# A fused attention and two-layer MLP kernel: another opening, another engine for one copy, and eight weight chunks prepared during attention

## Chip, cores and metric

The kernel runs on one core of one Trainium2 chip. The metric is the device time of one execution in microseconds; the median of three runs of the kernel before is 671.48 us (669.37 to 672.0).

## What is computed

The reference, cut to what matters (B = 2, H = 8, S = 768, D = 64, six hash bits):

```python
q_bits = (einsum('bhsd,dk->bhsk', q, proj) > 0)          # the same for k
mask = q_bucket[:, :, :, None] == k_bucket[:, :, None, :]
scores = where(mask, scale * q @ k.T, -1e9)
attn = softmax(scores); x = (attn @ v), heads side by side # 1536 x 512
h = x @ w_in;  y = (h * tanh(softplus(h))) @ w_out         # 512 -> 2048 -> 512
h = y @ w2_in; s = h * softmax(h)
out = layer_norm(s) * g_ln @ w2_out                        # 512 -> 1024 -> 512
```

The four weight matrices arrive as 64-bit floats. Every product is made of parts (a high part and a rest), so that the result has the precision of 32-bit floats.

## The kernel before

**Stages.** Sixteen heads are handled in eight pairs; each head has six tiles of 128 queries by 768 keys, 96 tiles in all. For a pair, `load_qk` reads q and k, `qk_split` and `qk_rest` (GpSimd) cut them into two parts, `qk_turn` (line 1114, TensorE) transposes them, and `qk_evac` (line 1130) copies them from PSUM into the operand A with ScalarE. q is needed a second time, as the first 64 rows of the operand B: `qk_again` (line 1122) copies the same two PSUM banks again, with ScalarE too, while k's part of B comes by a DMA from A (`qk_copy`). `bits` (TensorE) multiplies A by the projection, whose two parts are the tiles `ph` and `pl`; `signs` (line 1166, VectorE) turns the result into signs, and `bits_in` sends them by DMA into the last 12 rows of B, two DMAs a head. With A and B, `scores` makes four matmuls a tile; then come `row_max`, `row_bias` (VectorE), `exps` (ScalarE), a split and a transposition by DMA or by TensorE, and `weigh`, 18 matmuls with v.

The first pair is special. Its q and k are loaded head by head (`load_first`), and ScalarE (`first_high`) and VectorE (`first_low`) cut them, not GpSimd.

After attention, the first layer runs in 48 units (`up`, 12 matmuls of 512 columns; `mish`, five VectorE operations among others; `down_high` and `down_low`, 12 matmuls). Its tokens come transposed from `turn_x`. Units 0 to 4 use the first ten weight chunks, two a unit. The second layer works on twelve blocks of tokens.

**Weights.** They come in 48 chunks of 512 KB. A chunk is loaded by SP's queue (`w_load`, line 695) into one of two raw buffers, and `w_steps` (line 702) converts it: one ScalarE operation (line 708), four on VectorE (lines 710, 712, 714, 716), then the high part by ScalarE (line 721) and the rest by GpSimd (line 723). The first `nconv=4` chunks have room from the start; the next ones get theirs once the score buffers are given back, that is when attention's scores are made.

**Order.** All five queues have an order fixed at build time. `program_order` lists the operations with what they read and write; each has a cost (`COST`) and a due time (`PHASE`, in tiles); `Order.run` plays a list schedule with them, and the kernel emits the instructions in that order. Each engine then executes its queue strictly in order. Transposed tiles and weight chunks, and the operands A, B, live in rings whose sizes the planner knows: `ns=17` slots of 3 KB a partition for the tiles, `hb=5` operand buffers.

The opening in `program_order`:

```python
for h in range(2):
    for o in range(2):
        dma(("load0", h, o), -200 + h, "load0_", ...)
for i in range(2):
    dma(("const", 1 + i), -200, "const1", (), [("pj", i)])
```

Of the kernel before, what the change touches and what calls it, by code (L numbers as in the profile page):

```python
# [9 lines left out]
F32 = mybir.dt.float32  # L10
# [21 lines left out]
    score=3.35, max=20.58, bias=-41.09, exp=15.90, hi=38.27, lo=17.83, tdma=-17.31, tr0=9.66, thi0=-4.77,  # L32
    tlo0=10.96, tr1=11.10, thi1=34.69, tlo1=-13.57, weigh=18.21, norm0=14.45, norm1=-19.21, norm2=-18.99,
    load=9.76, vload=18.36, split0=-28.52, rest0=7.87, split1=21.38, rest1=13.25, turn=-1.67, evac=-13.71,
    copy=-20.07, bits0=0.84, bits1=5.16, sign=1.45, bdma=18.25, vmax=21.88, vs0=-7.99, vs1=-38.96, vs2=-32.92,
    vs3=2.95, vs4=-18.77, vs5=24.66, vs6=21.48, vs7=18.09, vs8=-29.73, vh=36.55, vl=-0.60, first=-10.47,
    turn_=28.58, evac_=34.57, copy_=-15.70, bits_=16.40, sign_=37.45, bdma_=19.08, vload_=-49.04, vmax_=44.13,
    vs_=-10.86, vh_=21.48, vl_=-28.42, second=83.83, wload=30.72, w0=22.26, w1=-4.27, w2=-0.69, w3=-21.85,
    w4=35.81, w5=1.29, w6=-6.70, wpace=-25.03, wat=161.08, wlate=-523.98, turngap=0.35, x0_=-1.63, x1_=4.53,
    x2_=17.68, load_=-22.95, const0=6.26, begin0=-1.50, vs8_=11.76, outlag=-10.05, up=-22.50, a0=23.29,  # L40
    a1=31.43, a2=29.92, a3=28.02, a4=-26.04, a5=-5.08, a6=25.14, a7=32.44, a8=34.92, a9=-7.34, a10=23.68,
    da=-13.05, db=-11.20, ky0=73.43, ky1=29.52, x0=20.32, x1=-16.34, x2=-11.42, sy0=19.47, sy1=20.33,
    u2=-10.02, n0=23.50, n1=0.20, n2=-4.13, n3=13.94, n4=24.34, n5=19.25, n6=-17.42, n7=-0.19, n8=32.85,
    n9=9.81, n10=14.27, n11=20.09, n12=-5.13, n13=21.63, t2=-30.92, l0=-7.19, l1=7.73, d2=22.76, ot=25.03,
    od=-2.50, wloadL=72.31, w0L=-5.19, w1L=12.35, w2L=42.25, w3L=-36.78, w4L=62.43, w5L=-4.37, w6L=-15.41,
    begin1=-37.18, begin2=-25.15, begin3=-15.47, const1=34.72, const3=-15.20, load0_=6.26,
# [4 lines left out]
    score=0.7, max=0.865, bias=0.14, exp=0.878, hiA=0.733, hiD=0.469, lo=1.596, tr=0.325, thi=0.371, tlo=0.469,  # L51
    weigh=0.533, norm0=0.075, norm1=0.106, norm2=0.469, split=0.915, rest=1.79, turn=0.5,
    evacA=0.691, evacD=0.865, bits=0.69, sign=0.985, vmax=0.87, vs0=0.11, vs1=0.2, vs2=0.11,
    vs=0.07, vs8=0.884, vh=0.733, firstA=0.413, firstD=0.469, w0=0.52, w1=0.602, w2=0.602,
    w3=0.602, w4=0.602, w5=0.52, w6P=1.225, w6D=0.663, x0=0.434, x1=0.478, x2=0.602,
    up=0.68, a0=0.478, a1=0.335, a2=0.602, a3=0.613, a4=0.52, a9=0.52, a10=1.225, da=0.453, db=0.2265,
    sy0=0.52, sy1=0.602, u2=1.36, n0=1.131, n1=1.091, n2=0.069, n3=0.075, n4=1.196, n5=0.069, n6=1.133,
# [13 lines left out]
COLD = 14.0  # L71


class Order:
# [60 lines left out]
    def run(self):  # L135
# [14 lines left out]
        free = dict(BEGIN)  # L150
# [49 lines left out]
        for _ in range(n):  # L200
            best = None
            for e, line in queue.items():
                cand = []
                for r, i in line:
                    r = max(r, free[e])
                    if ops[i][7]:
                        r = ring(i, r)[0]
                        if r is None:
                            continue
                    cand.append((r, due[i], i))  # L210
                if not cand:
                    continue
                first = min(cand)[0]
                pick = min((c for c in cand if c[0] <= first + self.slack), key=lambda c: c[1:])
                if best is None or pick[0] < best[0]:
                    best = (pick[0], e, pick[2])
            at, e, i = best
            o = ops[i]
            queue[e] = [x for x in queue[e] if x[1] != i]
            for tok, name, m, k in ring(i, at)[1]:  # L220
                place[tok] = k
                held[name][k:k + m] = [tok] * m
            for tok in o[7]:
                if tok[0] in taken:
                    taken[tok[0]].append(tok)
            start[i] = at
            if o[8] is not None:
                hw = max(at + 0.05, hw) + o[2]
                begin = max(hw + 0.65, wire)
                wire = done[i] = begin + o[8]  # L230
                if e == "SP":
                    free[e] = begin + 0.85 if o[0][0] == "tdma" else hw
                else:
                    free[e] = at + 0.05
            else:
# [3 lines left out]
                free[e] = done[i] = at + o[2] * (2 if e == "PE" and at < COLD else 1)  # L239
# [28 lines left out]
def program_order(pairs, tiles, routes, evac, chunks, wide, due, rings, stores, slack, queues=(), pooled=0,  # L268
                  gates=(0, 0, 0, 0), early=8, attention_only=False, split="G", again="A"):
# [11 lines left out]
    def start():  # L281
        dma(("const", 0), -200, "const0", (), [("cs",)])
        op(("begin", 0), A, 0.2, -200, "begin0", [("cs",)], [("ident",)])
        for h in range(2):
            for o in range(2):
                dma(("load0", h, o), -200 + h, "load0_", (), [(("r%d", "rr%d")[h] % o, 0)])
        for i in range(2):
            dma(("const", 1 + i), -200, "const1", (), [("pj", i)])
# [12 lines left out]
    def prep(n):  # L301
# [6 lines left out]
        for h in range(2):  # L308
            th = t0 if n else h * due["second"]
            for o in range(2):  # L310
                sp = ("sp%d" % o, n) if n else ("f", o, h)
                if not n:
                    op(("first", 0, h, o), A, COST["firstA"], th, "first", [(("r%d", "rr%d")[h] % o, 0)], [sp])
# [7 lines left out]
                if again and not o:  # L321
                    op(("evac", n, h, 2), A if again == "A" else V, COST["evac" + again], d, "evac" + f, [s],
                       [("B", n, h, 0)])
# [73 lines left out]
    def chunk(i, base, slot, reads):  # L397
# [3 lines left out]
        dma(("wload", i), base, "wload" + q, [("wg", i - 1)] + reads, [wr], 0, (("bdma", 0, (0,), 0, 1),))  # L401
# [171 lines left out]
def lsh_attention_moe_kernel(  # L573
# [15 lines left out]
    nconv=4,  # L589
# [9 lines left out]
    ns=17,  # L599
    early=5,  # L600
    hb=5,
# [8 lines left out]
    again="A",  # L610
# [511 lines left out]
    def qk_again(p, h):  # L1122
        dst = second(p, h, 0)[0:64].rearrange("p (a n) -> p a n", a=2)
        src = two_banks("st", p, h, 0)[0:64, :, 0:NH]
        if again == "A":
# [155 lines left out]

    def const_in(i):
# [23 lines left out]

    nc.gpsimd.memset(ones, 1.0)
# [4 lines left out]
    for w in v_t:  # L1312
        nc.gpsimd.memset(w[:, :, :, 0, D:D + 1], 1.0)
    nc.gpsimd.memset(ph.bitcast(F32), 0.0)
# [7 lines left out]
        bank=(8, dict(s=2, st=2, sb=2, sv=1, t=1, o=1, tx=1, h=1, q=1, wq=1, y0=1, y1=1, y2=1, y3=1, h2=2, t2=2, o2=1)),  # L1322
# [3 lines left out]
                          early, split=split, again=again)  # L1326
    keys = order.run()
    do = dict(
        load=load_qk, load0=load_first, split=qk_split, rest=qk_rest, const=const_in, begin=begin,
# [39 lines left out]
```

## Time and profile before

| what | value |
|---|---|
| median of three runs | 671.48 us |
| the profiled execution's own time | 670.35 us |
| its span, first to last instruction | 668.5 us |
| TensorE busy | 632.3 us (95%) |
| VectorE busy | 540.1 us (81%) |
| ScalarE busy | 445.3 us (67%) |
| GpSimd busy | 338.1 us (51%) |
| mean granted TensorE clock | 0.978 |
| the first score matmul and the last one start at | 18.5 and 222.6 us |

Busy times are of one execution. In the profile PE is TensorE, PEld its weight loads, DVE VectorE, ACT ScalarE, POOL GpSimd and SPq the queue of SyncE, which issues the DMAs. A matmul's recorded length overlaps the next one's, so the distance between the starts of two matmuls is what one takes. A clock of 1.00 is 2.4 GHz and 0.50 is 1.2 GHz.

### The profile page before, as it was taken

Reading aid. Unit: us, or ns where it says so; the run is one execution under the profiler, and the core shown is the slowest. Engines: PE = TensorE matmul, PEld = TensorE weight load, DVE = VectorE, ACT = ScalarE, POOL = GpSimd, SP = SyncE. Lnnn points to the kernel's source line nnn. Section 1 sums busy time; section 2 is a strip of 40 time slices with the busy share of each in tenths; the row PEclk is TensorE's granted clock in tenths of the full one; section 3 lists DMA queues with packets and bytes.
Section 4 is the critical chain, followed back from the end, with each engine's and each line's share of the span. In section 5 each row is a group of like instructions: output and inputs, shape, how many; then the busy total and the mean of one; then the engine's idle time right before and its main releaser. Section 6 shows DMA issues by size and latency. Waiting matters only on the chain.

```text
span 668.5 us, 12185 instructions
## 1 busy us (share of the span) xinstructions
PE 632.3 (95%) x4520; PEld 522.9 (78%) x4520; DVE 540.1 (81%) x1113; ACT 445.3 (67%) x718; POOL 338.1 (51%) x261
## 2 busy tenths in 40 slices
PE   5899899999989988799999999999999999999997
PEld 4788798887978866588777777887778888888886
DVE  3777869788799899999999999999998596545440
ACT  5889989999999856666666666655556265443341
POOL 4678867869568555466666665444566200000000
PEclk9879979999999999989999999999999999999999
DMA  6959869898999943322333221121120000000011
GB/s 173 234 145 178 192 144 181 172 194 163 149 189 190 198 115 122 95 95 73 95 103 95 86 92 60 63 70 56 64 95 1 1 0 18 16 32 17 16 49 48
DMA packets 125148, 68.11 MB, mean 102 GB/s; under 512 B 103584, under 2 KB 118048, under 8 KB 125088
## 3 DMA queue, kind: packets, MB, share of 16 engines
q1 hardware_dynamic: 125088, 67.33, 42.0%
q8 instruction: 35, 0.57, 0.4%
q14 instruction: 25, 0.20, 0.1%
HBM read 34.68 MB, written 3.15 MB: 57 GB/s over the span
## 4 chain that ended last, share of the span: by engine, by line
PE 53%; DVE 19%; ACT 5%; issue 5%; DMA 1%; POOL 1%; ACTq 0%; DVEq 0%; POOLq 0%
PE banks L815 4%; PE banks L817 4%; PE banks L816 4%; PE banks L871 4%; PE banks L872 4%; PE banks L876 4%; PE banks L920 3%; PE banks L924 3%; PE banks L986 3%; PE banks L984 3%; PE banks L921 3%; PE banks L985 3%; DVE mx L1202 3%; PE banks L1195 3%; DVE a L833 2%
## 5 line engine op out<-in xcount | busy, mean ns | idle before, releaser
L1244 POOL TENSOR_TENSOR store<-store 128x768 f16<-128x768 f32 x64 | 104.5, 1651 | 25.5 <-ACT store L1222 23.7
L1202 DVE TENSOR_REDUCE mx<-banks 128x1 f32<-128x768 f32 x96 | 90.5, 950 | 23.8 <-PE banks L1195 22.1
L849 POOL TENSOR_TENSOR n<-c,a 128x512 f32<-128x512 f32 x48 | 62.8, 1308 | 82.7 <-DVE a L845 73.9
L1211 ACT ACTIVATE store<-banks,mx 128x768 f32<-128x768 f32 x96 | 93.7, 995 | 6.4 <-DVE mx L1207 5.0
L815 PE MATMUL banks<-xh,w 128*128 128x512 f32 x192 | 78.7, 410 | 7.0 <-DVE xl L804 4.8
L871 PE MATMUL banks<-gh,w 128*128 128x512 f32 x192 | 76.1, 396 | 4.4 <-ACT gh L854 4.4
L817 PE MATMUL banks<-xh,w 128*128 128x512 f32 x192 | 76.2, 397 | 0.6 <-POOL w L723 0.6
L816 PE MATMUL banks<-xl,w 128*128 128x512 f32 x192 | 76.1, 396 | 0.2 <-DVE xl L804 0.2
L872 PE MATMUL banks<-gh,w 128*128 128x512 f32 x192 | 75.5, 393 | 0.0
L857 POOL TENSOR_TENSOR gl<-n,gh 128x512 fp32r<-128x512 f32 x48 | 62.9, 1309 | 18.9 <-ACT gh L854 18.9
L839 ACT ACTIVATE a<-n,two 128x512 f32<-128x512 f32 x48 | 34.7, 722 | 46.5 <-DVE n L835 46.5
L1262 PE MATMUL banks<-v,store 128*128 128x65 f16 x576 | 61.5, 195 | 3.3 <-DVE store L1239 1.8
L1195 PE MATMUL banks<-A,A 128*128 128x384 f32 x192 | 58.7, 387 | 4.3 <-ACT store L1211 4.1
L723 POOL TENSOR_TENSOR w<-wf,w 128x512 fp32r<-128x512 f32 x40 | 51.7, 1293 | 21.1 <-ACT w L721 20.1
L1264 PE MATMUL banks<-v,store 128*128 128x65 f16 x576 | 61.0, 193 | 0.5 <-DVE store L1239 0.5
L1263 PE MATMUL banks<-v,store 128*128 128x64 f16 x576 | 61.3, 196 | 0.0
L1262 PEld LDWEIGHTS <-store 128*128 128x128 f16 x576 | 53.8, 97 | 6.1 <-issue 4.3
L1263 PEld LDWEIGHTS <-store 128*128 128x128 f16 x576 | 54.1, 98 | 3.0 <-issue 2.6
L1264 PEld LDWEIGHTS <-store 128*128 128x128 f16 x576 | 54.2, 100 | 0.6 <-DVE store L1239 0.6
L876 PE MATMUL banks<-gl,w 128*128 128x512 f32 x192 | 53.7, 391 | 0.0
L1222 ACT ACTIVATE store<-store 128x768 f16<-128x768 f32 x64 | 52.8, 852 | 1.1 <-PE banks L1264 0.9
L815 PEld LDWEIGHTS banks<-xh,w 128*128 128x128 f32 x192 | 36.2, 188 | 21.6 <-DVE a L845 6.7
(123 smaller groups left out, 1715.9 us busy)
## 6 DMA issues: line engine op xcount, KB each, us to landing
wr<-in_moe_w_in_dram SPq DMA_DIRECT2D x24, 512.0 KB
wr<-in_moe_w_out_dram SPq DMA_DIRECT2D x24, 512.0 KB
vr<-in_v_dram SPq DMA_DIRECT2D x8, 384.0 KB
B<-A SPq DMA_DIRECT2D x16, 192.0 KB
out_dram<-ot SPq DMA_DIRECT2D x12, 256.0 KB
q<-in_q_dram SPq DMA_DIRECT2D x7, 384.0 KB
k<-in_k_dram SPq DMA_DIRECT2D x7, 384.0 KB
B<-bits SPq DMA_DIRECT2D x32, 36.0 KB
```

The lines of the kernel that those rows point to most:

```text
L815: nc.tensor.matmul(h, lhsT=wh[:, ks], rhs=xh, start=(kk == 0), stop=False)
L816: nc.tensor.matmul(h, lhsT=wh[:, ks], rhs=xl, start=False, stop=False)
L817: nc.tensor.matmul(h, lhsT=wl[:, ks], rhs=xh, start=False, stop=(kk == KD - 1))
L871: nc.tensor.matmul(y, lhsT=wh[:, os], rhs=g_t[u][0], start=first, stop=False)
L872: nc.tensor.matmul(y, lhsT=wl[:, os], rhs=g_t[u][0], start=False, stop=False)
L876: nc.tensor.matmul(y, lhsT=wh[:, os], rhs=g_t[u][1], start=False, stop=last)
L1202: nc.vector.reduce_max(m[:, 1:2], two_banks("s", t)[:, :, 0:NH], axis=AX.XY, negate=True)
L1211: nc.scalar.activation(kept("e", t).rearrange("p (a n) -> p a n", a=2), two_banks("s", t)[:, :, 0:NH], AF.Exp, bias=m[:, 3:4], scale=m[:, ...
L1244: nc.gpsimd.tensor_tensor(p16[:, 1], kept("e", t), p16[:, 0], op=ALU.subtract)
L1262: nc.tensor.matmul(o, lhsT=pt[:, 0, kc, :], rhs=vh, start=(kc == 0), stop=False)
L1263: nc.tensor.matmul(o[:, 0:D], lhsT=pt[:, 0, kc, :], rhs=vl, start=False, stop=False)
L1264: nc.tensor.matmul(o, lhsT=pt[:, 1, kc, :], rhs=vh, start=False, stop=(kc == NC - 1))
```

## The change

- **Opening.** DMA order: the constants, q and k of head 0, the two copies of the projection, then q and k of head 1. ScalarE may cut head 1's q only after it has begun k's copy of head 0. TensorE first does 20 matmuls of 192 columns on the zeroed tile `ph` (`warm`), for which GpSimd zeroes `ph` first.
- **q's second copy** (`again="VV"`) goes to VectorE for both heads of every pair; in the first pair it is listed behind k's copy.
- **Weights.** `nconv=8`: eight chunks have room from the start. The first four loads (`soon=4`) may be issued behind the loads of pair 1, not only behind the first signs. To make room, `ns` goes from 17 to 15 and `hb` from 5 to 4.
- **Planner.** Nearly all due times are new, some costs are changed by a few per cent, and the time for which the planner counts TensorE as slow goes from 14 to 5 us. So the order of all queues is another one.

```diff
@@ program_order: start, prep, chunk
         for h in range(2):
             for o in range(2):
-                dma(("load0", h, o), -200 + h, "load0_", (), [(("r%d", "rr%d")[h] % o, 0)])
-        for i in range(2):
-            dma(("const", 1 + i), -200, "const1", (), [("pj", i)])
+                dma(("load0", h, o), -200 + h, "load0_", (), [(("r%d", "rr%d")[h] % o, 0)], 0,
+                    [("const", 2)] if h else [])
+            for i in range(0 if h else 2):
+                dma(("const", 1 + i), -200, "const1", (), [("pj", i)], 0, [("load0", 0, 1)])
+        op(("warm",), T, COST["warm"], -200, "warm", [], [("warm", 0)])
...
-                    op(("first", 0, h, o), A, COST["firstA"], th, "first", [(("r%d", "rr%d")[h] % o, 0)], [sp])
+                    op(("first", 0, h, o), A, COST["firstA"], th, "first", [(("r%d", "rr%d")[h] % o, 0)], [sp], 0,
+                       [("evac", 0, 0, 1)] if h else [])
...
-                if again and not o:
-                    op(("evac", n, h, 2), A if again == "A" else V, COST["evac" + again], d, "evac" + f, [s],
+                if again and (o if n == 0 else not o):
+                    g = again[h]
+                    op(("evac", n, h, 2), A if g == "A" else V, COST["evac" + g], d, "evac" + f, [("st", n, h, 0)],
                        [("B", n, h, 0)])
...
-        dma(("wload", i), base, "wload" + q, [("wg", i - 1)] + reads, [wr], 0, (("bdma", 0, (0,), 0, 1),))
+        dma(("wload", i), base, "wload" + q, [("wg", i - 1)] + reads, [wr], 0,
+            (("load", 1, 1) if i < soon else ("bdma", 0, (0,), 0, 1),))
@@ parameters
-    nconv=4,
+    nconv=8,
-    ns=17,
+    ns=15,
-    hb=5,
+    hb=4,
-    again="A",
+    again="VV",
+    soon=4,
@@ new, and the zeroing moved
+    def warm():
+        for _ in range(20):
+            nc.tensor.matmul(bank("warm", 0)[:, 0:192], lhsT=ph[:, 0:128], rhs=ph, start=True, stop=True)
...
+    nc.gpsimd.memset(ph.bitcast(F32), 0.0)
     nc.gpsimd.memset(ones, 1.0)
...
-    nc.gpsimd.memset(ph.bitcast(F32), 0.0)
```

## Rows read from the trace of the kernel before

**Rows 1.** Stages: length, busy of PE, PEld, DVE, ACT, POOL; clock, DMA share, GB/s

```profile
0.00:18.40 18.40, 11.50 (x67) 8.12 (x67) 6.02 (x19) 11.23 (x19) 7.32 (x22) 0.91 0.68 189
18.40:50.00 31.60, 28.68 (x207) 24.41 (x206) 25.60 (x65) 26.21 (x37) 23.85 (x18) 0.84 0.73 181
50.00:100.00 50.00, 46.81 (x554) 41.17 (x551) 37.36 (x105) 45.48 (x63) 39.24 (x27) 0.90 0.87 172
100.00:180.00 80.00, 77.27 (x1033) 68.60 (x1033) 67.20 (x181) 77.34 (x110) 59.01 (x40) 1.00 0.89 175
180.00:222.90 42.90, 39.24 (x581) 35.22 (x579) 41.93 (x108) 42.36 (x63) 30.20 (x19) 1.00 0.97 179
222.90:250.00 27.10, 23.93 (x299) 20.25 (x297) 24.34 (x47) 18.36 (x32) 15.77 (x12) 1.00 0.66 157
250.00:290.00 40.00, 31.89 (x139) 24.06 (x138) 39.39 (x66) 24.83 (x42) 20.80 (x17) 0.96 0.33 105
290.00:410.00 120.00, 119.09 (x507) 93.45 (x505) 117.41 (x192) 76.25 (x130) 78.81 (x62) 1.00 0.29 93
410.00:530.00 120.00, 119.01 (x512) 95.56 (x512) 110.13 (x173) 65.19 (x110) 63.10 (x48) 1.00 0.14 49
```

**Rows 2.** Busy time in two microseconds of the stretch at low clock

```profile
84.00:86.00 2.00, 2.00 (x7) 2.00 (x8) 1.69 (x7) 1.89 (x3) 1.37 (x1) 0.50 1.25 283
```

**Rows 3.** Timeline of the first 19 us (start, length, engine, line, operation)

```profile
2.13 0.43 SPq L1039 DMA_DIRECT2D q<-in_q_dram  x1
...
4.80 1.76 PE L1120 MATMUL banks<-identr,sp 128*128 128x128 f32 x12 [4.80 <-DVE sp L1110]
...
5.67 0.52 ACT L1106 ACTIVATE sp<-q 128x384 fp32r<-128x384 f32 x1 [0.98 <-DMA q<-in_q_dram]
...
8.20 1.49 ACT L1137 ACTIVATE A<-banks 128x768 fp32r<-128x768 f32 x2
...
10.33 0.52 PE L1161 MATMUL banks<-A,ph 128*24 128x384 f32 x1
...
10.65 0.52 PE L1161 MATMUL banks<-A,pl 128*24 128x384 f32 x1
...
11.27 1.06 DVE L1169 TENSOR_SCALAR bits<-banks,cs 24x768 fp32r<-24x768 f32 x1 [1.36 <-PE banks L1161]
...
11.73 0.34 PE L1161 MATMUL banks<-A,ph 128*24 128x384 f32 x1
...
11.91 0.34 PE L1161 MATMUL banks<-A,pl 128*24 128x384 f32 x1
...
12.37 1.70 SPq L1177 DMA_DIRECT2D B<-bits  x2
...
12.96 1.22 PE L1120 MATMUL banks<-identr,sp 128*128 128x128 f32 x12
...
15.67 1.00 PE L1120 MATMUL banks<-identr,sp 128*128 128x128 f32 x6 [1.49 <-POOL sp L1099]
...
18.47 0.97 PE L1195 MATMUL banks<-A,A 128*128 128x384 f32 x2
```

**Rows 4.** Weight loads on SP's queue from 223 to 290 us, first and last

```profile
223.59 0.57 SPq L699 DMA_DIRECT2D wr<-in_moe_w_in_dram  x1
...
284.32 0.34 SPq L699 DMA_DIRECT2D wr<-in_moe_w_out_dram  x1
```

**Rows 5.** Waits between 223 and 292 us (total, times, longest us)

```profile
PE banks L815 <- DVE xl L804: 4.8, 3, 1.8
```

**Rows 6.** Instruction groups: busy us and mean ns behind the bar

```profile
L716 DVE SCALAR_TENSOR_TENSOR wf<-wr,banks 128x512 int32<-128x512 int32 x48 | 32.6, 679 | 0.0
...
L1137 ACT ACTIVATE A<-banks 128x768 fp32r<-128x768 f32 x32 | 25.6, 809 | 8.1 <-PE banks L1120 8.0
...
L1126 ACT ACTIVATE B<-banks 64x768 fp32r<-64x768 f32 x16 | 12.7, 795 | 0.0
...
L1169 DVE TENSOR_SCALAR bits<-banks,cs 48x768 fp32r<-48x768 f32 x7 | 7.4, 1062 | 0.2
```

More of the change, by code (lines that the diff above doesn't have):

```diff
@@ L31 @@
 PHASE = dict(
[L32 to L46, printed above, removed]
+    score=2.89, max=21.69, bias=-20.48, exp=-7.37, hi=37.60, lo=-74.88, tdma=47.79, tr0=9.51, thi0=14.05,
@@ new lines @@
+    tlo0=2.17, tr1=10.84, thi1=28.04, tlo1=16.57, weigh=17.46, norm0=29.45, norm1=6.67, norm2=-77.92,
+    load=19.06, vload=18.96, split0=-188.88, rest0=28.62, split1=-216.02, rest1=37.27, turn=-44.19,
+    evac=-204.06, copy=-27.06, bits0=-103.88, bits1=-136.11, sign=51.37, bdma=40.93, vmax=21.86, vs0=-271.50,
+    vs1=9.08, vs2=-210.73, vs3=-129.45, vs4=-56.64, vs5=-127.12, vs6=-290.81, vs7=144.62, vs8=-328.13,
+    vh=70.16, vl=45.25, first=63.48, turn_=6.48, evac_=195.41, copy_=-35.91, bits_=94.54, sign_=168.35,
@@ new lines @@
+    bdma_=-9.06, vload_=-304.47, vmax_=171.56, vs_=87.04, vh_=-22.87, vl_=-122.68, second=35.58, wload=28.78,
+    w0=-41.17, w1=84.02, w2=-26.10, w3=26.15, w4=31.29, w5=19.05, w6=290.37, wpace=-25.50, wat=214.24,
+    wlate=-420.19, turngap=-246.21, x0_=-6.98, x1_=-173.02, x2_=44.49, load_=10.81, const0=66.52,
+    begin0=-146.26, vs8_=150.21, outlag=-5.17, up=-162.02, a0=-14.23, a1=40.52, a2=25.54, a3=14.48, a4=30.07,
+    a5=-71.43, a6=11.38, a7=-135.40, a8=-17.97, a9=76.71, a10=229.81, da=51.52, db=-112.61, ky0=101.10,
@@ new lines @@
+    ky1=110.82, x0=37.16, x1=118.52, x2=72.93, sy0=21.03, sy1=8.66, u2=24.00, n0=-198.44, n1=78.28, n2=130.92,
+    n3=-69.22, n4=-178.31, n5=-31.52, n6=140.09, n7=224.60, n8=-279.51, n9=-111.63, n10=-196.61, n11=-61.38,
+    n12=-275.68, n13=3.09, t2=-8.41, l0=-92.90, l1=222.42, d2=202.96, ot=-141.26, od=-47.76, wloadL=-156.21,
+    w0L=2.89, w1L=23.01, w2L=229.21, w3L=-26.73, w4L=229.00, w5L=-89.36, w6L=-69.41, begin1=-117.25,
+    begin2=-102.32, begin3=76.98, const1=123.70, const3=67.06, load0_=-1.00,
@@ L47 @@
 )
 COST = dict(
[L51 to L56, printed above, removed]
@@ L57 @@
-    sy0=0.52, sy1=0.602, u2=1.36, n0=1.131, n1=1.091, n2=0.069, n3=0.075, n4=1.196, n5=0.069, n6=1.133,
+    score=0.79, max=0.865, bias=0.18, exp=0.878, hiA=0.733, hiD=0.469, lo=1.61, tr=0.33, thi=0.371, tlo=0.469,
+    weigh=0.555, norm0=0.075, norm1=0.106, norm2=0.531, split=0.8, rest=1.79, turn=0.515,
+    evacA=0.691, evacV=0.865, warm=3.2, bits=0.7, sign=0.985, vmax=0.87, vs0=0.11, vs1=0.2, vs2=0.11,
+    vs=0.07, vs8=0.884, vh=0.733, firstA=0.413, firstD=0.469, w0=0.56, w1=0.602, w2=0.602,
@@ L58 @@
+    w3=0.602, w4=0.783, w5=0.52, w6P=1.253, w6D=0.663, x0=0.47, x1=0.478, x2=0.602,
+    up=0.7, a0=0.494, a1=0.335, a2=0.602, a3=0.613, a4=0.52, a9=0.52, a10=1.25, da=0.464, db=0.2265,
+    sy0=0.52, sy1=0.602, u2=1.39, n0=1.131, n1=1.091, n2=0.069, n3=0.075, n4=1.196, n5=0.069, n6=1.133,
     n7=0.188, n8=0.094, n9=0.069, n10=0.13, n11=0.069, n12=0.069, n13=0.723, t2=0.87, d2=2.72,
@@ L70 @@
 BEGIN = dict(PE=0.6, Activation=1.9, DVE=0.65, Pool=2.0, SP=0.55, X=0.0)
-COLD = 14.0
+COLD = 5.0
 class Order:
@@ L238, in run @@
                     port[e] = at + o[2]
-                free[e] = done[i] = at + o[2] * (2 if e == "PE" and at < COLD else 1)
+                free[e] = done[i] = at + o[2] * (2 if e == "PE" and at < COLD and o[0][0] != "warm" else 1)
             got.append(i)
@@ L268, in program_order @@
 def program_order(pairs, tiles, routes, evac, chunks, wide, due, rings, stores, slack, queues=(), pooled=0,
-                  gates=(0, 0, 0, 0), early=8, attention_only=False, split="G", again="A"):
+                  gates=(0, 0, 0, 0), early=8, attention_only=False, split="G", again="AA", soon=0):
     order = Order(rings, stores, slack, due)
@@ L1124, in qk_again @@
         src = two_banks("st", p, h, 0)[0:64, :, 0:NH]
-        if again == "A":
+        if again[h] == "A":
             nc.scalar.activation(dst, src, AF.Copy, scale=SC)
@@ L1321, in lsh_attention_moe_kernel @@
     stores = dict(
-        bank=(8, dict(s=2, st=2, sb=2, sv=1, t=1, o=1, tx=1, h=1, q=1, wq=1, y0=1, y1=1, y2=1, y3=1, h2=2, t2=2, o2=1)),
+        bank=(8, dict(warm=1, s=2, st=2, sb=2, sv=1, t=1, o=1, tx=1, h=1, q=1, wq=1, y0=1, y1=1, y2=1, y3=1, h2=2, t2=2, o2=1)),
         store=(ns, dict(e=1, p16=1, pt=1)),
@@ L1325, in lsh_attention_moe_kernel @@
     order = program_order(NP, NC, routes, evac, nconv, is_wide(w1_in), due, rings, stores, slack, queues, pooled, gates,
-                          early, split=split, again=again)
+                          early, split=split, again=again, soon=soon)
     keys = order.run()
     do = dict(
-        load=load_qk, load0=load_first, split=qk_split, rest=qk_rest, const=const_in, begin=begin,
+        warm=warm, load=load_qk, load0=load_first, split=qk_split, rest=qk_rest, const=const_in, begin=begin,
         first=lambda i, h, o: (first_high, first_low)[i](h, o),
```

## The prediction

> **What bounds the kernel now.** I first read the busy time by stage [rows 1]. From 290 us on TensorE stands still for less than 1 us in each 120 us: the change touches little there. Before 290 us no engine is full all the time. In the attention stage (18.4 to 222.9 us) PE is busy 192.0 of 204.5 us (28.68 + 46.81 + 77.27 + 39.24), ACT 191.4 and DVE 172.1 (25.60 + 37.36 + 67.20 + 41.93). So DVE has some 32 us to spare, ACT 13. In the entry to the first layer (222.9 to 290 us) it is DVE that is full, 39.39 of 40.0 us from 250 on, while PE waits 3.2 + 8.1 us. The opening has 6.0 us of DVE work in 18.4 us.
>
> Part of PE's busy time is slow. The granted clock of the two stages between 18.4 and 100 us is 0.84 and 0.90 [rows 1]. At two levels, 2.4 and 1.2 GHz, that is 32% of 31.6 us and 20% of 50 us at the lower one, some 10 us each; 84 to 86 us is such a piece, at 0.50 [rows 2]. At half rate 20 us cost PE 10 us, if nothing else holds it.
>
> The opening is a chain in the timeline [rows 3]. Head 0's q and k are transposed from 4.80 to 6.56 us. ACT then cuts head 1's q and k first (5.67 to 6.68 us), so that k's copy of head 0 ends only near 9.0 us (the first half of the pair at 8.20). Eight projections follow, 0.32 us apart (10.33, 10.65), the signs at 11.27, two DMAs from 12.37 to 14.07, and the first scores at 18.47. At 11.73 and 11.91 the same projections stand 0.18 us apart: until about 11 us PE ran at the lower level, although the granted clock reads 1.00 there [rows 3]. Between the DMAs and the scores PE's queue holds transposes of pair 1, one of which waits 1.49 us for GpSimd at 15.67 [rows 3].
>
> The entry is bound by weights. Four loads are issued before 222.9 us, twelve from 223.59 to 284.32 [rows 4], while units 0 to 4 need ten chunks in all. PE's largest wait there is for VectorE's half of the transposed tokens, 4.8 us [rows 5]: it stands in a queue that conversions fill.
>
> **The change, step by step.**
>
> Opening. Without head 1's cuts ahead of it, q's copy fits behind the first six transposes and k's starts when all twelve end, 6.6 us, and ends at 7.4 (0.8 us, as half of the pair at 8.20), 1.6 us earlier. The projections after it took 2.3 us (9.0 to 11.27); at 0.18 us apart 1.4, at the old rate 2.3. Signs 1.06, two DMAs 1.70. For the landing I have bounds only: below 3.1 us, which a load of 192 KB took from the end of its issue at 2.56 to its use at 5.67 [rows 3], and above nothing; I take 2 us, nearer to the load. Sum: 7.4 + 1.4 + 1.1 + 1.7 + 2.0 = 13.6 us for the first scores, 4.9 us earlier. Ends: 16.1 us if PE's order still holds the scores as long as now, and 11.6 if the bits land at once.
>
> The 20 matmuls on zeros go before 4.80 us, where PE has nothing to do. A projection has 384 columns and takes 0.32 us at the lower level, so 192 columns take 0.16 and 20 of them 3.2 us. If each took its recorded 0.52 us they would take 10.4 and delay the chain by some 7; the distance of starts is what rows show for a stream, so I take 3.2, which fits ahead of 4.80 if the tile is zeroed by 1.6 us. Their gain is at most what the clock is worth in the chain: 0.9 us on projections, counted above, and 0.5 on transposes (1.76 against 1.22 us for twelve at 12.96 [rows 3]), not counted. Moving the constants ahead of head 1 delays that head by two issues, some 1.2 us, while head 0 computes. One early weight load (512 KB, 1.9 us at the 283 GB/s of [rows 2]) may stand before the bits; it costs 0 to 1.9 us, taken as 0, since the loads of pair 1 stand there as well now.
>
> q's second copy. 16 copies of 795 ns leave ACT, 12.7 us. On DVE the nearest row is the signs, also 768 elements from PSUM, 1062 ns [rows 6]. Starts are closer than lengths: 66 instructions fill 39.39 us [rows 1], 0.60 us each where rows say 0.68 [rows 6], so 0.97 a copy and 15.5 us in all. The lower bound is ACT's own 0.795, 12.7 us.
>
> The copy of A and the copy of B read the same PSUM banks, until now on one engine. No row shows two engines' copies of one bank, so the sum counts no wait between them; the last rival does. The Trainium skill, "PSUM — Partial Sum Buffer", section "PSUM bank collisions raise a hardware error", says that two engines must not access one bank at once, reads included; by that rule one copy always waits for the other, and the sum would be the last rival's.
>
> Four more chunks converted in attention: 16 VectorE steps of 0.60 us, 9.6 us, that leave the entry. SP's queue gets four more loads among its DMA transposes, 0.34 to 0.57 us each [rows 4], 2.3 us at most in 204, taken as 0. GpSimd's four operations meet an engine busy 152.3 of 204.5 us [rows 1].
>
> Attention's end. DVE's work up to it becomes 6.0 + 172.1 + 15.5 + 9.6 = 203.2 us, of which some 4 precede the first scores. The 199.2 us that remain take 205.4 us if DVE is 97% full, as it was in the last 42.9 us of the stage (41.93, 97.7%), where conversions already filled it; over the whole stage it was 84%, but there it had less to do. 13.6 + 205.4 = 219.0, 3.9 us earlier. At 97.7% it is 5.4 earlier, at 93% 4.9 later. ACT loses 12.7 us and gets eight operations, shorter than the 0.81 us of a wider copy [rows 6], 6.5 at most; and PE's 192.0 include the slow pieces, so neither is the later one.
>
> Entry. DVE gives 9.6 us back; PE can gain its 11.3 us of waits and the 1.6 that 0.96 of clock costs in 40 us [rows 1]. I take 7.5: the smaller, less part of the wait for transposed tokens, which stay. Ends: 3 and 12.9.
>
> Smaller rings. Two tile slots of 17 and one operand buffer of 5 less shorten the lead of scores over `weigh`. Nothing shows the price; PE's waits from 50 to 222.9 us are 9.6 us [rows 1], and it could add as much again, or nothing. I take nothing: a head's operands need two buffers a pair, and four still hold this pair and the next. The new order of the queues cannot be worked out; bounded by the same waits, it is 0 with ± 9.6.
>
> Sum: 670.35 - 3.9 - 7.5 = 658.95 us against the profiled execution's 670.35 (span 668.5 and 1.85 around it). The median shown is 1.13 above that execution, so **660.0 us** for the median.
>
> **Rivals.**
>
> *More gain, by the clock.* If the 20 us at the lower level do not come back, PE gets up to 10 us; where DVE is the limit that is worth little. With 7 of them, 653 us. For it: PE's gaps go before those pieces, and the opening's gap (1.49 us at 15.67) is among those removed. Against: DVE fuller means more short waits for PE.
>
> *The chunks come no earlier.* SP's queue serves transposes first, and a load whose due time is late stays late; only 4 loads left in 222.9 us. Then the entry stays, and the start alone gives 3 to 4 us: 667.5.
>
> *VectorE becomes the bound, and the time longer.* In attention DVE has 199.2 us of work; at 90% full it takes 221.3 and the stage ends at 234.9, 12 later, with the entry's 7.5 gained: 676. It decides below 92%: at 199.2 / 216.8 the end, 230.4, eats the whole gain of 7.5. For it: each score tile waits for `row_max` in the same queue, and 84% is what the stage has held. Against: 97.7% at its end.
>
> *VectorE stands behind ScalarE* at each second copy: up to 0.81 us in each of the 14 after the first pair [rows 6], with its whole queue behind it, 11.3 us: 671. For it: the banks are the same. Against: VectorE's queue may reach the copy when ScalarE's is long done.
>
> **Chances and range.** Forecast 0.52, clock 0.14, late chunks 0.14, VectorE as the bound 0.13, VectorE behind ScalarE 0.07. The measurement can tell about 0.5% from no change, 3.4 us: faster is below 668.1. The forecast, the clock and nearly half of the late chunks lie there, 0.72; slower than 674.8 is most of the VectorE case, 0.12; the rest, 0.16, is no change. The range, 650 to 672, leaves out the best of the clock case (0.06) and the slower end (0.14).
>
> **What would show it.** Right: first scores near 13.6 us; projections 0.18 us apart from the start; the eighth weight load issued before the last scores; PE's idle time from there to unit 6 below 5 us instead of 11.3; DVE 95% busy or more in attention. Wrong: first scores behind 16 us, DVE at 90% and PE waiting for `row_max` at the same time, or a last score later than 222.6 us, which the entry would have to pay back.

## The result, and the profile after

| | before | after |
|---|---|---|
| median, same chip, 4 executions each | 670.93 us (669.37 to 672.0) | 661.34 us (660.74 to 663.35) |
| ratio, 95% interval | | 0.9864 [0.9834, 0.9895] |
| profiled execution, and its span | 670.35, 668.5 us | 663.35, 661.6 us |
| mean granted clock in it | 0.978 | 0.990 |
| last score matmuls on B begin at | 222.6 us | 231.9 us |

The forecast was 660.0 us, in a range of 650 to 672. The total is right; the way to it is not. The last scores come nine microseconds later, not four earlier, and the time comes back in the entry to the first layer. The stages first, cut where the scores of the changed kernel begin and end (the columns are those of [rows 1]):

```profile
0.00:14.60 14.60, 11.30 (x76) 9.62 (x76) 7.27 (x20) 7.26 (x13) 4.87 (x21) 1.00 0.70 197
14.60:50.00 35.40, 27.96 (x203) 22.08 (x203) 30.79 (x73) 29.19 (x41) 28.10 (x21) 0.95 0.89 204
50.00:100.00 50.00, 46.28 (x585) 40.06 (x584) 43.25 (x118) 42.54 (x60) 37.23 (x26) 0.93 0.83 176
100.00:180.00 80.00, 74.21 (x959) 64.25 (x959) 68.38 (x177) 68.50 (x96) 60.18 (x41) 0.98 0.89 169
180.00:231.90 51.90, 48.36 (x642) 41.85 (x642) 48.77 (x119) 49.23 (x74) 32.68 (x22) 1.00 0.87 177
231.90:250.00 18.10, 17.72 (x267) 15.15 (x266) 17.90 (x39) 14.48 (x25) 13.59 (x11) 1.00 0.78 191
250.00:290.00 40.00, 39.33 (x187) 32.12 (x186) 39.32 (x67) 27.57 (x49) 24.08 (x19) 1.00 0.23 71
290.00:410.00 120.00, 118.62 (x507) 93.33 (x506) 116.62 (x191) 72.55 (x126) 77.89 (x62) 1.00 0.28 88
410.00:530.00 120.00, 118.98 (x521) 96.54 (x520) 113.08 (x188) 68.81 (x120) 60.46 (x46) 1.00 0.16 53
```

Read the third number of the four attention rows: VectorE is busy 191.2 of 217.3 us, 88%. So it has much more to do than before (172.1 us), and still it is not full. PE stands still for 20.5 us there (12.5 before). From 250 to 290 us PE was busy 31.89 us [rows 1]; now it is 39.33. After 290 us the two kernels are alike.

To see where time is won I added up TensorE's progress: all matmuls that have begun by time t, each kind counted at the distance of its starts at full clock, without the matmuls on zeros. The difference to the kernel before, in us (plus is ahead; this is a sum over groups of instructions, no view of the profile, and good to about 1 us; "late chunks" and the others are runs told below, "copy from A" is the second run of that edit):

```
t                     20    40   100   220   300   380   420   600
after               +1.4  +0.1  -0.9  -6.5  +6.4  +6.8  +5.1  +6.6
late chunks         +0.5  -1.1  -1.1  -3.7  +0.3  -0.4  -2.8  -2.3
small rings alone    0.0  -0.1  +0.3  -8.9  -7.8  -8.3 -15.3 -20.3
one slot more       -0.5  -1.1  -0.9  -8.0  +2.1  +3.2  -6.1  -7.8
copy from A         +1.6  -0.5  +1.5  -2.7 +11.7 +12.1 +10.8 +12.7
```

The first line closes: 6.6 us ahead at 600 us, against 6.9 us between the spans. The opening's lead is used up by 40 us, attention loses 6.5, the entry wins 12.9, and the rest nothing.

The opening, in the timeline (it answers to [rows 3]):

```profile
1.04 4.58 PE L1291 MATMUL banks<-ph 128*128 128x192 f32 x20 [1.04 <-POOL ph L1318]
...
5.42 1.39 PE L1127 MATMUL banks<-identr,sp 128*128 128x128 f32 x12
...
6.35 1.51 ACT L1144 ACTIVATE A<-banks 128x768 fp32r<-128x768 f32 x2 [0.30 <-PE banks L1127]
...
7.19 0.95 DVE L1135 TENSOR_SCALAR B<-banks 64x768 fp32r<-64x768 f32 x1 [0.86 <-ACT A L1144]
...
8.20 0.35 PE L1168 MATMUL banks<-A,ph 128*24 128x384 f32 x1 [1.39 <-DVE B L1135]
...
8.39 0.33 PE L1168 MATMUL banks<-A,pl 128*24 128x384 f32 x1
...
9.55 0.95 DVE L1055 TENSOR_REDUCE am<-vr 128x1 f32<-128x768 f32 x1 [0.22 <-DMA vr<-in_v_dram]
...
10.42 1.06 DVE L1176 TENSOR_SCALAR bits<-banks,cs 24x768 fp32r<-24x768 f32 x1
...
11.50 1.70 SPq L1184 DMA_DIRECT2D B<-bits  x2
...
13.53 1.22 PE L1127 MATMUL banks<-identr,sp 128*128 128x128 f32 x12
...
14.59 0.58 PE L1202 MATMUL banks<-A,A 128*128 128x384 f32 x2
```

The steps are those of the forecast, in its order, but two of them wait for something that it did not count. The projections are 0.17 to 0.19 us apart from the first on, but begin at 8.20 instead of 7.4 us. The signs begin at 10.42, as VectorE ends a reduction over v (line 1055) that its queue has ahead of them. The first scores follow at 14.59 instead of 13.6, directly behind twelve transposes of pair 1 that PE's queue has ahead of them.

### The profile page after: what moved, and what is told of

Read it like the earlier page. It is cut to its first block, busy times and chain, and to the rows that moved or that the text cites. A ratio compares the mean times of both kernels' runs of the same rounds, so it can differ in the third digit from the quotient of the medians.

```text
span 661.6 us, 12270 instructions
## 1 busy us (share of the span) xinstructions
PE 630.6 (95%) x4540; PEld 521.3 (79%) x4540; DVE 549.8 (83%) x1129; ACT 432.7 (65%) x702; POOL 339.1 (51%) x261
## 4 chain that ended last, share of the span: by engine, by line
PE 46%; DVE 16%; ACT 5%; issue 4%; DMA 3%; POOL 1%; SPq 0%; DVEq 0%; ACTq 0%; POOLq 0%
PE banks L822 3%; PE banks L824 3%; PE banks L823 3%; PE banks L991 3%; PE banks L931 3%; PE banks L993 3%; PE banks L928 3%; PE banks L927 3%; PE banks L992 3%; PE banks L878 3%; PE banks L883 3%; PE banks L879 3%; DVE a L852 2%; DVE a L840 2%; DVE a L850 2%
## 5 line engine op out<-in xcount | busy, mean ns | idle before, releaser
L1218 ACT ACTIVATE store<-banks,mx 128x768 f32<-128x768 f32 x96 | 92.3, 994 | 14.4 <-PE banks L1271 5.2
L822 PE MATMUL banks<-xh,w 128*128 128x512 f32 x192 | 76.6, 399 | 2.5 <-DVE a L852 1.7
L824 PE MATMUL banks<-xh,w 128*128 128x512 f32 x192 | 75.7, 394 | 0.0
L883 PE MATMUL banks<-gl,w 128*128 128x512 f32 x192 | 72.7, 396 | 0.0
L1202 PE MATMUL banks<-B 76*128 76x384 f32 x192 | 50.9, 347 | 0.0
```

What stands on the lines that cost most here:

```text
L822: nc.tensor.matmul(h, lhsT=wh[:, ks], rhs=xh, start=(kk == 0), stop=False)
L824: nc.tensor.matmul(h, lhsT=wl[:, ks], rhs=xh, start=False, stop=(kk == KD - 1))
L883: nc.tensor.matmul(y, lhsT=wh[:, os], rhs=g_t[u][1], start=False, stop=last)
L1202: nc.tensor.matmul(s[:, half, 0:NH], lhsT=opnd[nm, p, j, 0][:, cc], rhs=opnd[nm, p, j, 1][:, hs], start=(i == 0), stop=(i == 1),)
L1218: nc.scalar.activation(kept("e", t).rearrange("p (a n) -> p a n", a=2), two_banks("s", t)[:, :, 0:NH], AF.Exp, bias=m[:, 3:4], scale=m[:, ...
```

## The experiments

All but two begin from the changed kernel. What matters in reading them is whether the planner's order stayed. The edits of the copy and of the zeros leave PE's order as it is, late chunks leave it up to 177.51 us: they show the worth of a part. The others are planned anew from early on.

**The changed kernel again.** No edit.

> The changed kernel itself, unaltered, on one chip with the next three, so that they can be set against it: 0.983 to 0.990 of the time of the kernel before.

664.34 us (658.98 to 665.01), 0.9890 [0.9833, 0.9948], as expected. Together with the first four executions: about 0.986 to 0.989 of before.

```profile
L1202 PE MATMUL banks<-A,A x192: 331/340/689, 14.3 to 232.8; 128*128 128x384 f32 x192
```

Its last scores on the first part begin at 232.8 us, those of the first profiled execution at 231.5. With the two runs that follow, which keep PE's order too (230.9 and 229.5), the end of attention scatters over some 3 us, and a smaller difference shows nothing.

**q's second copy back on ScalarE, in the same place of the order.**

```diff
-        if again[h] == "A":
+        if True:
```

> The changed kernel with its queues in the same order, but q's second copy is executed by ScalarE again. If the copies on VectorE are what makes attention end 9 us later than before (VectorE waits 7.9 us for ScalarE's copy of the same banks, ScalarE 5.3 us for VectorE's), the last scores start 4 to 9 us earlier than at 231.5 us and the median falls from 661.3 to 653 to 658 us. If the new order and the conversions are the cause, ScalarE, which gets 12.7 us back, is the fuller engine: last scores between 230 and 236 us, median 661 to 667 us.

662.35 us (661.84 to 663.0), 0.9911 [0.9890, 0.9933]. One window over its attention, and the matmuls of the scores on the first part and on B (first and last start):

```profile
14.60:231.50 216.90, 196.85 (x2388) 168.75 (x2386) 179.63 (x471) 197.45 (x280) 157.97 (x107) 0.96 0.87 178
```

```profile
L1202 PE MATMUL banks<-A,A x192: 331/340/689, 14.7 to 230.9; 128*128 128x384 f32 x192
L1202 PE MATMUL banks<-B x192: 332/338/522, 15.2 to 231.3; 76*128 76x384 f32 x192
```

VectorE has 11.6 us less to do (179.63 against 191.19 us) and ScalarE 8.0 more, and the last scores move by 0.6 us. So the copy on VectorE, and its waits for ScalarE, are not what makes attention end later than before. That no engine's load sets the end is not shown by this: the work only changed its engine, and ScalarE, now busy 91% of the time, may hold what VectorE held. The copy's new engine brings nothing that could be told from the changed kernel.

**No matmuls on zeros.**

```diff
-        for _ in range(20):
+        for _ in range(0):
```

> The changed kernel without the 20 matmuls on zeros, all else in the same order. If they raise TensorE's clock ahead of the chain, head 0's projections stand 0.32 us apart again instead of 0.18, the first scores come 1 to 2 us later than at 14.6 us, and the median is 661 to 664 us. If the zeros are worth nothing, the projections keep 0.18 us and the median stays at 661 us; if the zeros only hold the transposes back (they end at 5.62 us, transposes begin at 5.42), the scores come up to 0.8 us earlier.

660.79 us (659.39 to 661.27), 0.9882 [0.9855, 0.9910]: no difference. The timeline shows that they do what they are for, and that the first scores come 0.3 us later without them, not the 1 to 2 us expected; the last scores come at 229.5:

```profile
8.26 0.52 PE L1168 MATMUL banks<-A,ph 128*24 128x384 f32 x1
8.58 0.52 PE L1168 MATMUL banks<-A,pl 128*24 128x384 f32 x1
...
10.42 1.06 DVE L1176 TENSOR_SCALAR bits<-banks,cs 24x768 fp32r<-24x768 f32 x1 [0.41 <-PE banks L1168]
...
13.88 1.21 PE L1127 MATMUL banks<-identr,sp 128*128 128x128 f32 x12
...
14.93 0.58 PE L1202 MATMUL banks<-A,A 128*128 128x384 f32 x2
```

```profile
L1202 PE MATMUL banks<-A,A x192: 331/340/648, 14.9 to 229.5; 128*128 128x384 f32 x192
```

Without them the projections of head 0 are 0.32 us apart, as in [rows 3]; but they begin at 7.66 us instead of 8.20, because the transposes begin at 4.68 and not at 5.42, behind the zeros. The zeros take back more than half of what they give (0.54 us of start for 0.97 us of projections). The rest does not reach the signs, which begin at 10.42 us in both timelines: here they wait for the projections, with the zeros for the reduction over v. The 0.3 us come by another way, the transposes of pair 1 ahead of the scores (13.88 here, 13.53 with the zeros).

**Chunks 4 to 7 loaded only behind the last scores.**

```diff
-            (("load", 1, 1) if i < soon else ("bdma", 0, (0,), 0, 1),))
+            (("score", pairs * span - 1) if 4 <= i < 8 else ("load", 1, 1) if i < soon else ("bdma", 0, (0,), 0, 1),))
```

> The changed kernel, its order planned again with one more condition: chunks 4 to 7 may be loaded only behind the last scores. If the early chunks are what shortens the entry, TensorE's idle time from the last scores to the end of unit 5 is 8 us or more instead of 1.1, attention ends 2 to 6 us earlier, and the median is 666 to 671 us. If the gain after 232 us comes from the new due times, the median stays within 3 us of 661.

673.8 us (672.38 to 681.33), 1.0105 [1.0046, 1.0164], some 12 us above the two runs before it on the same chip. PE's order is the changed kernel's up to a pair of matmuls on B that begins at 177.51 us here and at 180.85 in the changed kernel. Behind it, for the last 50 us of attention and for the entry, the order is another one as well, and the 12 us hold both. Its last scores, and its busy time in the entry and behind it:

```profile
L1202 PE MATMUL banks<-A,A x192: 331/340/687, 15.6 to 227.2; 128*128 128x384 f32 x192
```

```profile
231.50:290.00 58.50, 50.33 (x412) 40.40 (x411) 53.42 (x91) 35.35 (x61) 31.32 (x25) 0.97 0.49 122
290.00:400.00 110.00, 106.04 (x449) 82.36 (x448) 106.72 (x175) 67.69 (x118) 73.32 (x58) 1.00 0.31 96
```

Attention ends 4.3 us earlier; PE then stands still for 8.2 us up to 290 and 4.0 us behind. But the 4.3 us are not the price of four chunks. The pair of matmuls at which the orders part, in the changed kernel, here, and in the run without zeros, which has all eight chunks early; and the changed kernel's first conversion of a chunk that is late here:

```profile
180.85 0.52 PE L1202 MATMUL banks<-B 76*128 76x384 f32 x2
177.51 0.52 PE L1202 MATMUL banks<-B 76*128 76x384 f32 x2
177.84 0.52 PE L1202 MATMUL banks<-B 76*128 76x384 f32 x2
177.54 0.67 ACT L715 ACTIVATE wf<-wr 128x512 f32<-128x512 f32 x1 [1.42 <-DMA wr<-in_moe_w_in_dram]
```

So 3.3 of the 4.3 us were there before those chunks could cost anything, and the run without zeros has 3.0 of them. The profiled execution of the changed kernel lost them: from 121 to 131 us its clock is 0.83 and PE is busy for 8.71 us, where both others have 1.00 and 9.7. From the pair to the last scores, late chunks win 1.0 us on the changed kernel and 2.0 on the run without zeros. That is what is left for the four chunks in attention, and for the other order with them.

Against late chunks, the changed kernel loses 2.8 us of TensorE's progress up to 220 us, wins 8.9 from there to 300 and 2.8 more by 600. Late chunks themselves go from -3.7 to +0.3 in the entry, 4.0 us against before that come without the chunks. Whether the 8.9 are the chunks' or the order's, this run can't tell: PE's longest wait up to 290 us is for `gh` of `mish`, 4.2 us, which badly ordered runs below show too:

```profile
PE banks L878 <- ACT gh L861: 4.2, 2, 3.6
```

All runs together can tell. PE's idle time in some 60 us behind the last scores is 11.2 us before, 11.4 with the small rings alone and 8.2 here, with four early chunks each. With eight it is 4.6 (the kernel before with eight early chunks), 5.5 (old due times), 3.7 (old opening), 0.1 (one slot more) and 1.0 us (the changed kernel, both executions), though the orders differ as much:

```profile
222.90:283.00 60.10, 48.93 (x413) 38.78 (x411) 56.73 (x101) 40.09 (x69) 31.90 (x24) 1.00 0.49 132
234.00:294.00 60.00, 48.58 (x371) 38.83 (x370) 51.02 (x90) 34.90 (x60) 30.82 (x24) 0.97 0.46 121
241.10:301.00 59.90, 55.30 (x483) 45.49 (x482) 53.02 (x95) 39.17 (x68) 33.78 (x25) 0.97 0.48 119
239.80:300.00 60.20, 60.15 (x435) 49.28 (x433) 58.30 (x100) 38.87 (x68) 33.95 (x26) 1.00 0.35 90
```

(The kernel before, the small rings alone, the same with eight early chunks, one slot more.) So the early chunks are the part that shortens the entry.

**VectorE copies q from A in SBUF, not from the banks.**

```diff
-            nc.vector.tensor_scalar(dst, src, SC, None, op0=ALU.mult)
+            nc.vector.tensor_copy(second(p, h, 0)[0:64], opnd["A", p, h, 0][0:64])
...
+    for n in range(NP):
+        for h in range(2):
+            i, j = keys.index(("evac", n, h, 2)), keys.index(("evac", n, h, 0))
+            if i < j:
+                keys.insert(j, keys.pop(i))
```

> The changed kernel, but VectorE makes q's second copy from the first copy (operand A in SBUF) and not from the PSUM banks; a second copy that stood ahead of the first one in the order now stands behind it. If the common banks cost time (each engine waits for the other's copy), ScalarE's 5.3 us of waits for VectorE go, a copy takes about 0.5 us instead of 0.95, the last scores start 3 to 8 us earlier and the median is 654 to 659 us. If VectorE's load and the banks are not what limits attention, it stays at 660 to 663 us.

656.3 us (656.03 to 660.7), 0.9836 [0.9799, 0.9872]. The median lies where the banks as a cost were expected; the last scores, 2.2 us earlier, do not, and the repetition further below takes the median back. For comparison the waits of the changed kernel in attention (who waits for whom: total, times, longest), then this run's:

```profile
DVE B L1135 <- ACT A L1144: 7.9, 7, 2.3
PE banks L1202 <- ACT store L1218: 7.6, 9, 2.4
ACT A L1144 <- DVE B L1135: 5.3, 6, 1.6
```

```profile
DVE B L1135 <- ACT A L1144: 17.3, 12, 4.2
```

In the changed kernel VectorE's copy and ScalarE's of the same banks stand behind each other, 7.9 us one way and 5.3 the other: the waits of the last rival. The Trainium skill, "PSUM — Partial Sum Buffer", section "PSUM bank collisions raise a hardware error", says that two engines must not access one bank at once; the trace agrees in that it shows one waiting for the other, 13 times. But the wait is not the price: with the copy from A, VectorE waits longer, 17.3 us, and ScalarE doesn't wait for it any longer, and the last scores come at 229.3, not later.

**The kernel before with eight early chunks and the small rings, on its old due times; and with the small rings alone.**

```diff
-    nconv=4,
+    nconv=8,
...
-    ns=17,
+    ns=15,
...
-    hb=5,
+    hb=4,
```

> The kernel before with room for eight early chunks and the smaller rings that this needs (15 tile slots, 4 operand buffers), planned with its own old due times and costs; old opening, copies on ScalarE. If the early chunks are the change's main gain, TensorE's waits between 222 and 290 us fall from 11.3 to under 4 us, the last scores come 2 to 6 us later than at 222.6 us, and the time is 0.985 to 0.994 of before. If the gain needs the new due times, the waits stay above 7 us and the ratio lies between 0.995 and 1.005.

691.08 us, 1.0284 [1.0216, 1.0351], last scores at 240.7 us: slower than either reading had it. The second run has the lower two of the three edits.

> The kernel before with 15 tile slots for 17 and 4 operand buffers for 5 and nothing else, planned with the old due times. If smaller rings cost nothing, as the prediction took it, 0.997 to 1.003. If they are why attention ends later, the last scores come 3 to 6 us later and the ratio is 1.004 to 1.009.

689.53 us, 1.0282 [1.0237, 1.0328], last scores at 233.7 us, again outside both readings. Between these two runs the four early chunks change nothing in the total: what the entry wins (PE idle for 4.6 us instead of 11.4) is lost in attention, which ends 7 us later, at a lower clock (0.968 in the profiled execution against 0.978). By itself the second run reads as "smaller rings cost 19 us". The table of progress contradicts it: 8.9 us are lost in attention, but 12 more behind 300 us, where no head and no score tile is left to need those rings. PE's waits between 290 and 660 us:

```profile
PE banks L871 <- ACT gh L854: 5.8, 4, 2.5
PE banks L815 <- DVE a L845: 3.6, 4, 1.6
```

The kernel before has the same two waits for 1.2 and 0.7 us; it stood still for 1.9 us in the 240 us from 290 on [rows 1].

**The changed kernel with before's due times and costs.** All else stays as in the changed kernel.

```diff
-PHASE = dict(score=2.89, ...
+PHASE = dict(score=3.35, ...
-COST = dict(score=0.79, ...
+COST = dict(score=0.7, ...
```

> The changed kernel in all its parts (opening, zeros, copies on VectorE, eight chunks, smaller rings), but planned with the due times and costs of the kernel before. If the named parts carry the gain, 0.985 to 0.992. If the new due times carry half of it or more, 0.992 to 1.000, with the loss spread over attention.

688.83 us, 1.0275 [1.0213, 1.0337]. Its scores:

```profile
L1201 PE MATMUL banks<-A,A x192: 331/339/688, 17.3 to 246.0; 128*128 128x384 f32 x192
```

All parts of the change without the new due times (and costs) make the kernel 2.8% slower, beyond both readings. Two explanations are left: the new times are better ones, or any times fit only the program that they were found for. The next run tells them apart.

**One tile slot more.** Nothing gets scarcer, the due times stay.

```diff
-    ns=15,
+    ns=16,
```

> The changed kernel with 16 tile slots instead of 15, planned again with the same due times: nothing gets scarcer, only the planner's order differs (PE's queue from its row 612 on). Ring theory (scarce slots cost time by themselves): equal or a little faster, 655 to 663 us, last scores at or before 231 us. Fit theory (the due times are fitted to one set of rings, and any other set unfits them): slower although a slot is added, 668 us or more, with the loss of TensorE's progress spread over the stages, as in the run with only the small rings (689.5).

677.21 us (676.43 to 680.84), 1.0134 [1.0084, 1.0184]: slower than the changed kernel by 2.5 to 2.7% (its two ratios above), with one buffer more. PE's queue is another one from its row 612 on. The last scores come at 239.3 us, and then between 290 and 530 us:

```profile
PE banks L878 <- ACT gh L861: 8.8, 7, 3.6
```

The changed kernel has this wait once, for 0.8 us. Busy time from 380 to 420 us, first of this run, then of the changed kernel:

```profile
380.00:420.00 40.00, 32.71 (x131) 24.11 (x130) 37.77 (x60) 24.01 (x41) 20.65 (x17) 0.96 0.28 93
```

```profile
380.00:420.00 40.00, 38.99 (x164) 29.83 (x164) 39.23 (x64) 25.38 (x44) 22.17 (x18) 1.00 0.25 87
```

6.3 us of PE's time are gone in a stage which the slot does not touch; what the edit changed there is the order in which ScalarE and VectorE serve `mish`. So the ring theory falls for all that is lost behind attention: an edit that makes no buffer scarcer costs nearly as much as the edits that did, by the order that it unfits. In attention it is not tested: this run has small rings too, and by 220 us it is only 1.5 us behind the changed kernel.

**The opening of before in the changed kernel.** The four loads of heads 0 and 1 first, v's load behind the projection's copies, ScalarE free to cut head 1, no zeros.

```diff
-                dma(("load0", h, o), -200 + h, "load0_", (), [...], 0, [("const", 2)] if h else [])
-            for i in range(0 if h else 2):
-                dma(("const", 1 + i), -200, "const1", (), [("pj", i)], 0, [("load0", 0, 1)])
+                dma(("load0", h, o), -200 + h, "load0_", (), [...], 0, [("const", 0)])
+        for i in range(2):
+            dma(("const", 1 + i), -200, "const1", (), [("pj", i)])
...
-                       [("evac", 0, 0, 1)] if h else [])
```

> The changed kernel with the opening of before: all four loads of heads 0 and 1 ahead of the two copies of the projection, ScalarE free to cut head 1 at once, no matmuls on zeros. Theory that the opening's lead is used up before 40 us (TensorE's progress stood at 0.1 us against before there): first scores near 18.4 us, last scores within 3 us of 231.5, total within 3 us of the changed kernel (about 0.987 of before). Rival, that the 3.9 us of earlier first scores reach the end: total 3 to 5 us longer, about 0.993. Third, that the planner's order falls apart with any edit: 1.00 or more, lost in attention and not before 20 us.

682.68 us (681.08 to 685.94), 1.0212 [1.0169, 1.0255]; scores from 18.1 to 237.8 us. It is the third of the three: the planner's order changed in all queues, and some 20 us went against the changed kernel, most of it where the opening has no part (PE waits 5.7 us for `gh` behind 290 us, as in the runs above). It says nothing of what the opening is worth.

**Copy from A without zeros, and copy from A again, six executions each.** The edits are those above.

> VectorE copies q from operand A in SBUF (as in the run copy from A) and the matmuls on zeros are left out. If the zeros are worth nothing: within 0.3% of the next run. If the clock at the start matters: 2 us longer, first scores 0.5 us later or more.

659.7 us (657.9 to 664.24), 0.9872 [0.9834, 0.9911].

> The run copy from A once more, with more rounds, to set it beside the changed kernel. If VectorE's wait for ScalarE at the shared banks costs time (8 us of VectorE's and 5 us of ScalarE's waits in attention): 0.980 to 0.986 of before, 1 to 4 us under the changed kernel. If those waits are slack: the changed kernel's ratio, 0.986 to 0.989, within 1 us.

660.05 us (656.83 to 664.41), 0.9873 [0.9831, 0.9915].

```profile
L1202 PE MATMUL banks<-A,A x192: 331/340/690, 14.7 to 226.5; 128*128 128x384 f32 x192
```

The zeros are worth nothing here either. The copy from A ends the scores 5 us earlier than the changed kernel, at 226.5 us in this execution, and the span is 656.6 us; but its clock is 0.994 against 0.990, and in the first run of the same kernel the scores end at 229.3. Also the six times spread over 7.6 us, and their ratio and the changed kernel's cannot be told apart. Both beat the kernel before; which of the two is the better one is open.

## Why the prediction came out right

**Opening: right in its steps, wrong in its worth.** 14.59 us for 13.6. The evacuations take 6.35 to 7.86 us where the forecast let the second end at 7.4, and the projections wait 0.3 us more for VectorE's copy (8.14 us, its end). The signs wait for a reduction in VectorE's queue, which the sum did not have. The landing of the bits was not measured: issued by 13.20 us, they are first read by a matmul on B at 15.01, ahead of which no wait shows, so it took at most 1.8 us, inside the bounds; the first score matmuls, on A alone, do not need it. That PE's queue holds the scores back stood in the forecast only as its late end, 16.1 us. The whole lead of 3.9 us is gone at 40 us, and no run here shows that any of it reaches the end.

**Zeros: nothing in the total.** The sum had counted 0.9 us for faster projections. Those came, but the zeros took 4.58 us and not the 3.2 ahead of 4.80 that the step had, and pushed the transposes by 0.7; 0.3 us are left at the first scores.

**q's copy: the price right, the place wrong.** 16 copies at 947 ns are 15.1 us; the forecast had 0.97 and 15.5:

```profile
L1135 DVE TENSOR_SCALAR B<-banks 64x768 fp32r<-64x768 f32 x16 | 15.1, 947 | 12.6 <-ACT A L1144 8.8 <-PE banks L1127 3.8
```

**Attention's end: the step that failed.** It said that 199.2 us of VectorE's work, at 97% full, set the end at 219.0 us. There were 191.2 us of it, at 88%, and an end at 231.9. The share is below the 92% from which the third rival, VectorE as the bound, decides, and near the 90% and 234.9 us that it named. But its mechanism is not shown either: with 11.6 us taken off VectorE, 8.0 of them put on ScalarE, the end moved by 0.6 us, less than it scatters. The four chunks are worth 1 to 2 us of it. No single engine is full in this stage: PE is 91% busy, VectorE 88, ScalarE 87, each queue strictly in order, and each waits in turn for another (PE for the banks that `exps` frees, 7.6 us, where it was 4.1; not for `row_max`). Some 3 of the nine us were lost around 125 us in this execution alone. What remains came with the smaller rings or with the other order; since every edit of a ring makes a new order, the two were not told apart, and the cause of the longer attention stays open.

**New order "0 ± 9.6" and rings "0": the terms that were mis-sized.** The same program takes 688.83 us on the old due times and 664.34 on the new ones, on the same chip: 24 us; and a spare slot costs 2.5 to 2.7%, 16 to 18 us. The bound was taken from PE's waits in attention; but the order also sets the first layer, where the kernel before had no waits that could have shown it. They don't show in the total because the new due times suit the smaller rings, as the old ones don't. Whether the new times would also be the better ones for the kernel before was not tried.

**Entry: right in mechanism, too small.** The eighth load is issued before the last scores, at 229.02 us, and PE stands still for 1.05 us from the last scores to 286.5, where below 5 was asked:

```profile
171.72 0.58 SPq L706 DMA_DIRECT2D wr<-in_moe_w_in_dram  x1
...
229.02 0.57 SPq L706 DMA_DIRECT2D wr<-in_moe_w_out_dram  x1
```

```profile
231.90:286.50 54.60, 53.55 (x437) 44.36 (x436) 53.80 (x99) 39.10 (x68) 34.95 (x27) 1.00 0.41 109
```

```profile
PE banks L822 <- DVE a L852: 0.7, 1, 0.7
```

The wait for transposed tokens, 4.8 us in [rows 5], which the forecast kept in part, is not among PE's waits any more. The entry won 12.9 us of progress, the upper end of the step's 3 to 12.9; late chunks win 4.0 there without the chunks. That the chunks carry it is shown by the idle times above, in every order that was tried; how the 12.9 divide between chunks and order is not. The rival of chunks that come no earlier is refuted by the loads.

**The clock: a part, in the profiled pair above all.** Added up over windows of 1 us, the lower level cost 13.7 us of the execution before and 6.8 of the one after; the stages from 14.6 to 100 us are at 0.95 and 0.93, where before had 0.84 and 0.90 [rows 1]. Both stages are in attention, which ended later all the same. And other executions move: 25 of the kernel before, beside the later runs, have spans from 664.3 us at a clock of 0.990 to 671.9 at 0.982, with a mean clock of 0.986; eight of the changed kernel have 0.989. A straight line through those 25 gives 0.66 us of span for each us lost to the clock, so that 0.003 of 660 us, 2.0 us, is worth 1.3 us of the gain; this is a correlation, not an experiment.

**The sum.** 3.9 + 7.5 = 11.4 us were forecast for the profiled execution; -6.5 + 12.9 are 6.4, and the spans differ by 6.9. The median came nearer than its parts (661.34 for 660.0) since the other executions of the changed kernel were faster than the profiled one. Two errors, 10.4 us in attention and 5.4 in the entry, had opposite signs. They hang together by 1 to 2 us, the work of the chunks that leaves the entry for attention; that the rest nearly cancels is luck.

## What to carry to other kernels

Where a planner's due times are fitted to one program, an edit that makes it plan again measures the fit and not the edit: first measure a neutral edit (here one spare buffer, 2.6% slower), and trust only experiments that leave the order in place up to the point in question. A fill of 84% before is not to be taken for room up to 97%: with 19 us more to do, VectorE came to 88%, and the stage became 13 us longer, for reasons that were only in part found. What paid, in the changed kernel's order, was to move work out of a stage in which its queue is full, VectorE's conversions in the entry, into one where it costs less. And before a difference in one stage is put down to an edit, see whether it is there ahead of the first instruction that the edit concerns, and how far two executions of one kernel differ there.

## What was not expected of the hardware

The copy of q, 64 x 768 elements on VectorE, takes 947 ns out of the banks (`tensor_scalar`) and on average 744, 709 or 710 ns (three runs) out of SBUF (`tensor_copy`). The averages hide two kinds (shortest, median and longest, in ns):

```profile
L1135 DVE TENSOR_SCALAR B<-banks x16: 935/949/950, 7.2 to 188.5; 64x768 fp32r<-64x768 f32 x16
L1135 DVE CAST B<-A x16: 537/576/1498, 6.7 to 187.0; 64x768 fp32r<-64x768 f32 x16
```

Out of the banks all are alike. Out of SBUF 28 of 48 take 536 to 554 ns, and the 20 that take 0.6 to 1.5 us all run beside an operation of GpSimd (lines 1087, 1096, 1101, 1106). GpSimd's own cut of line 1101, at most 842 ns in the changed kernel, takes up to 1149 ns beside them. Why some copies beside GpSimd stay short was not tried.

Twenty matmuls of 192 columns on zeros took 4.58 us, 0.23 each, and the transposes behind them 1.39 us for twelve, between the 1.76 of a start without zeros and the 1.22 of [rows 3]; the granted clock reads 1.00 all the while, so in the first microseconds only the distance of starts tells the level.
